# A second Strassen level for the S4 B22 product of three gate-and-up pairs

## The chip, the cores and the metric

One core of a Trainium2 chip. The metric is device time in microseconds; the kernel before takes 1020.71 us (median of three runs, 1020.18 to 1020.84). TensorE (PE) multiplies, VectorE (DVE) adds and splits, ScalarE (ACT) copies, splits and computes the gelu, SyncE (SP) issues loads, GpSimd (POOL) issues stores.

## The reference

`x` is 2048 x 640, in float32:

```python
g = _sigmoid((x * gate_w).sum(-1, keepdims=True))
y = Cr @ (x @ Hr.T) - Ci @ (x @ Hi.T)              # branch A: real part of a 2-D DFT, by matrices
b = (_gelu(x @ w_gate) * (x @ w_up)) @ w_down      # branch B: hidden size 1728
out = g * y + (1 - g) * b
```

## The kernel before

Each float32 factor is split into a high and a low float32r part (`high` on ACT, `low` on DVE, line 81), and one product of 128x128 by 128x512 is `mm3`: three matmuls, lines 89 to 91, high by high, high by low, low by high. All large products go through a Strassen-Winograd scheme: sums T1 to T4 of blocks of x, sums S1 to S4 of blocks of the weights, and sums of the partial results.

Gate and up of branch B work on the hidden blocks in pairs. `k = p` counts pairs, `f = 2p + 1` and `f + 1` are the two weight blocks of a pair. Pairs 2 to 5 run through the generator `whole_pair`. The names in it: `X[i, tp]` and `Z[i, tp]` are PSUM banks for weight block i and half tp of the rows of x; `s1`, `s2` are tiles of 128x512 in SBUF with gate results and state, `s5` (two buffers) holds the up part. `va`, `xa_`, `ve`, `xe` and `za`, `ze` are the banks of a second Strassen level, in which the 2 x 2 grid of (weight block, half of x) is taken as a matrix again: J = 1 and 2 for A11 and A12, J = 3 for S1 T1. For a level J, `WP[J]` holds its weights (a11, a12, a22 and the sums s1 to s4), `b[J]` its x blocks (b11, b21, b22 and t1 to t4); t1, t2, t4 come from DRAM (`xtd[J]`) by `load_cross(J, i)` into tiles `xx`, t3 replaces a block of x that is no longer used. `m(ps, J, w, x)` is one product of a second level, `prod` two (the block's two halves), `fifth` one. A `seed` copies a bank into another (ACT, line 461), a `plus` adds (DVE, line 548), `state` copies X into s2 (ACT, line 137). After `gated_out` (gelu, multiply, stores: lines 707 to 714) and `up_out` (lines 720 to 726) a block's results go to DRAM.

The order of PE's work is that of the program (`in_order(PE)`). DVE and ACT take theirs from the framework's list scheduling, in program order as far as inputs are ready by its reckoning, plus edges made by hand: `mark(key)` remembers the last instruction, `behind(key)` puts the newest one behind it on its engine. The generator yields numbers u, and the loop around it puts the rest between: `chain_parts` (sums and splits of the S weights: tiles ws, wd), `fifth_parts` (sums s1 to s4 for J = 3: tiles fs, fh), `plain_parts` (tile wp), `next_pair` (the next pair's vs, vl, ve, vq), `extras` (sums for a later stage, and logits of the gate: tiles dr, xz), loads. `next_pair`'s first sums and the extras are behind the mark "dve".

Most SBUF tiles (4 KB a partition) rotate through one pool of 46 slots, of which the x blocks keep some 32; a load waits on SP until a slot is free. PSUM has eight banks. After pair 5 the K stage multiplies by w_down: step i needs the splits kl, kb..0l and kb..1l of step i.

## Time and profile before

| | |
|---|---|
| median of the runs | 1020.71 us |
| profiled execution, its own time | 1020.78 us |
| its span | 1019.0 us |
| PE busy | 1013.6 us, 4488 matmuls |
| DVE, ACT, POOL busy | 811.6, 494.9, 145.5 us |
| pairs 3, 4, 5 | from 190.2, 237.1 and 284.0 us on |
| K stage | from 331.1 us on |

In a timeline a row gives start and length in us, engine, line, operation, the tile written and those read (buffer numbers left out: `s` is any of s1, s2, s5, `px` any X bank), the shape, and in brackets how long the engine was idle before and who ended that. Rows overlap, since an engine begins an instruction while the one before ends, so the cost of one is best read from start to start.

### The profile page before, as it was taken

The page shows a single profiled execution, that of the slowest core. Times are in us where ns is not written, and L with a number is a line of the kernel's source. Part 1 is how long each engine was busy: PE and PEld are TensorE (multiplying, and loading weights), DVE is VectorE, ACT ScalarE, POOL GpSimd, SP SyncE. Part 2 cuts the span into 40 slices and gives each one's busy share as a digit, 9 for nine tenths or more (in the row PEclk, how much of TensorE's full clock was granted, in tenths as well). Part 3 has the DMA queues.
Part 4 walks back from the last instruction along what each step waited for, and adds up shares of the span by engine and source line. Part 5 has one row for each costly group of instructions (what it writes and reads, how often), then busy time and mean ns, then how long its engine had stood idle before and what let it go on. Part 6 is the DMA issues. An engine that isn't in the chain of part 4 may idle for free.

```text
span 1019.0 us, 13152 instructions
## 1 busy us (share of the span) xinstructions
PE 1013.6 (99%) x4488; PEld 835.3 (82%) x4488; DVE 811.6 (80%) x1148; ACT 494.9 (49%) x660; POOL 145.5 (14%) x259
## 2 busy tenths in 40 slices
PE   9999999999999999999999999999999999999998
PEld 7888888888888888887888888888888888888887
DVE  6988887978778939967898976878687769797777
ACT  5455455545365637456455443434443345455431
POOL 0113130212123100100010022002100200021013
PEclk9999999999999999999999999999999999999999
DMA  8358797959699978877866579657965878697748
GB/s 283 138 189 300 267 331 235 350 198 351 208 344 365 359 257 275 294 245 259 294 222 219 198 265 333 237 199 264 336 210 195 303 245 289 249 388 219 258 97 132
DMA packets 87795, 265.01 MB, mean 260 GB/s; under 512 B 11216, under 2 KB 19440, under 8 KB 87728
## 3 DMA queue, kind: packets, MB, share of 16 engines
q1 hardware_dynamic: 65392, 194.47, 56.0%
q0 software_dynamic: 22192, 69.50, 20.1%
q8 instruction: 35, 0.57, 0.2%
q14 instruction: 32, 0.26, 0.1%
q10 hardware_dynamic: 144, 0.20, 0.1%
HBM read 194.38 MB, written 69.75 MB: 259 GB/s over the span
## 4 chain that ended last, share of the span: by engine, by line
PE 87%; issue 8%; DVE 2%; POOL 1%; DMA 1%; ACT 1%; POOLq 0%; ACTq 0%; DVEq 0%
PE pX L89 4%; PE pX L90 4%; PE pX L91 4%; PE pL L89 3%; PE pL L90 3%; PE pL L91 3%; PE px L89 3%; PE px L91 3%; PE px L90 3%; PE pZ L89 2%; PE pZ L90 2%; PE pZ L91 2%; PE pV L89 2%; PE pV L90 2%; PE pV L91 2%
## 5 line engine op out<-in xcount | busy, mean ns | idle before, releaser
L78 ACT ACTIVATE ch<-csa 128x1024 fp32r<-128x1024 f32 x32 | 34.0, 1063 | 75.2 <-DVE csa L868 66.9
L81 DVE TENSOR_TENSOR cl<-cra,ch 128x1024 fp32r<-128x1024 f32 x32 | 39.2, 1224 | 28.8 <-ACT ch L78 23.4
L78 ACT ACTIVATE ch<-cra 128x1024 fp32r<-128x1024 f32 x32 | 33.9, 1060 | 57.0 <-PE pY L90 19.2
L81 DVE TENSOR_TENSOR cl<-crb,ch 128x1024 fp32r<-128x1024 f32 x32 | 39.1, 1223 | 13.5 <-ACT ch L78 11.4
L90 PE MATMUL pL<-cl,xah 128*128 128x512 f32 x128 | 49.8, 389 | 0.0
L91 PE MATMUL pL<-ch,xal 128*128 128x512 f32 x128 | 49.8, 389 | 0.0
L89 PE MATMUL pL<-ch,xah 128*128 128x512 f32 x128 | 49.3, 389 | 0.0
L78 ACT ACTIVATE ch<-crb 128x1024 fp32r<-128x1024 f32 x32 | 33.8, 1057 | 22.6 <-DVE cl L81 7.8
L81 DVE TENSOR_TENSOR cl<-csb,ch 128x1024 fp32r<-128x1024 f32 x32 | 39.2, 1225 | 2.0 <-ACT ch L78 0.5
L81 DVE TENSOR_TENSOR cl<-csa,ch 128x1024 fp32r<-128x1024 f32 x32 | 39.1, 1221 | 1.7 <-PE pL L90 0.7
L78 ACT ACTIVATE ch<-csb 128x1024 fp32r<-128x1024 f32 x32 | 34.0, 1064 | 10.3 <-DVE csb L871 6.4
L350 POOL DMA_DIRECT2D hA<-s x48 | 26.2, 546 | 83.1 <-DVE s L708 52.2
L707 ACT ACTIVATE s<-s 128x512 f32<-128x512 f32 x20 | 12.7, 633 | 49.1 <-DVE s L548 33.0
L81 DVE TENSOR_TENSOR kl<-kw,kh 128x1024 fp32r<-128x1024 f32 (+1 forms) x26 | 31.5, 1211 | 3.6 <-ACT kh L78 3.6
L78 ACT ACTIVATE kh<-kw 128x1024 fp32r<-128x1024 f32 (+1 forms) x26 | 27.2, 1046 | 7.9 <-DVE kw L926 4.7
L981 POOL DMA_DIRECT2D out<-ks x12 | 6.5, 543 | 167.1 <-DVE ks L980 166.5
L548 DVE TENSOR_TENSOR s<-s,px 128x512 f32<-128x512 f32 x12 | 8.2, 686 | 27.5 <-ACT s L630 25.9
L1343 POOL DMA_DIRECT2D uA<-c x8 | 4.3, 543 | 170.9 <-DVE c L1430 170.7
L350 POOL DMA_DIRECT2D hT<-s x48 | 26.0, 543 | 17.9 <-DMA hA<-s 3.1
L91 PEld LDWEIGHTS pL<-ch,xal 128*128 128x128 f32 x128 | 24.0, 188 | 5.0
L89 PEld LDWEIGHTS pL<-ch,xah 128*128 128x128 f32 x128 | 24.0, 188 | 5.0
L90 PEld LDWEIGHTS pL<-cl,xah 128*128 128x128 f32 x128 | 24.0, 188 | 5.0
(3089 smaller groups left out, 3471.4 us busy)
## 6 DMA issues: line engine op xcount, KB each, us to landing
cra<-in_ct SPq DMA_DIRECT2D x64, 512.0 KB, 4.0
crb<-in_ct SPq DMA_DIRECT2D x64, 512.0 KB, 4.8
xx<-xtd SPq DMA_DIRECT2D x42, 512.0 KB, 6.1
hA<-s POOLq DMA_DIRECT2D x48, 256.0 KB, 5.9
hT<-s POOLq DMA_DIRECT2D x48, 256.0 KB, 6.4
kr<-hA SPq DMA_DIRECT2D x24, 512.0 KB, 7.9
kr<-hT SPq DMA_DIRECT2D x24, 512.0 KB, 6.3
ux<-uA SPq DMA_DIRECT2D x24, 512.0 KB, 6.0
```

Source lines behind the costliest of these rows:

```text
L78: nc.scalar.activation(hi, raw, AF.Copy)
L81: nc.vector.tensor_tensor(lo, raw, hi.bitcast(F32), op=ALU.subtract)
L89: nc.tensor.matmul(ps, lh, rh, start=first, stop=False, skip_group_check=True)
L90: nc.tensor.matmul(ps, lh, rl, start=False, stop=False, skip_group_check=True)
L91: nc.tensor.matmul(ps, ll, rh, start=False, stop=last, skip_group_check=True)
L350: nc.gpsimd.dma_start(to[:, i], src)
L548: tt(a, a, c, op=ALU.add)
L707: nc.scalar.activation(s2, s2, AF.Gelu_apprx_tanh)
L981: nc.gpsimd.dma_start(out[2 * tp + t, e], src)
L1343: nc.gpsimd.dma_start(to[:, i], src)
```

## The change

For p = 3, 4, 5 the part of `whole_pair` behind u = 23 is replaced by `inner_two`. There S4 B22 gets a second level too, J = 4: its weights are S4 of both blocks and new sums `inner_parts(p, 4)`; its x blocks are block (2, 2) and its sums `xtd[4]`, loaded by three more `load_cross` a pair. The banks of J = 3 (`Z`) go on accumulating J = 4's products after s5 has taken its part, and two banks `wa`, `we` hold the shared partial results, which DVE adds into s2. To free two banks, the first block's A22 T4 product and the first half of `up_out` (`up_first`) run earlier; the copies of X into s5 therefore come first. p = 2 makes the sums for J = 4 (`cross_loads(4)`, `cross_sums(4)`, a split at u = 65), and its extras move. In pair 5 `gate_rows` moves from u = 47 to 56.

```diff
-    def fifth_parts(p, W0, W1):
-        a, b = W0["raw"], W1["raw"]
+    def inner_parts(p, J, W0, W1):
+        a, b = W0["raw"][J], W1["raw"][J]
...
+        streamed(3, "S1")
+        if p > 2:
+            yield from inner_two(p, m, prod, fifth, plus, gelu, state, streamed, X, Z, s1, s2)
+            return
...
+    def inner_two(p, m, prod, fifth, plus, gelu, state, streamed, X, Z, s1, s2):
+        f = 2 * p + 1
+        prod(X[0, 1], 0, "S3", "T3", 1)
+        za, ze = bank(f"pza{p}"), bank(f"pze{p}")
+        m(za, 3, "a11", "b11", True)
+        Z[0, 0] = seed(za, f"pz00{p}")
+        gelu(s1[1, 1])
+        m(ze, 3, "s1", "t1", True)
+        sz = copy(ze, f"sz{p}")
+        prod(X[1, 0], 1, "S2", "T2", 0)
+        state(1, 0)
+        yield 29
+        m(Z[0, 0], 3, "a12", "b21")
+        m(za, 3, "s2", "t2")
+        Z[0, 1] = seed(za, f"pz01{p}")
+        prod(X[1, 1], 1, "S2", "T2", 1)
+        state(1, 1)
+        mark("state")
+        yield 32
+        s5 = sumtile(f"s5{f}")
+        for tp in range(2):
+            nc.scalar.activation(s5[:, tp], X[0, tp], AF.Copy)
+            behind("state")
+        fifth(Z[0, 0], 0, "u5", 1, 0)
+        prod(X[0, 0], 0, "A22", "T4", 0)
+        fifth(X[0, 0], 0, "u5", 0, 0)
+        plus(s5[:, 0], Z[0, 0])
+        mark("dve")
+        up_first(X[0, 0], 0, p, s1[0, 0])
+        yield 36
+        m(Z[0, 1], 3, "s4", "b22")
+        m(za, 3, "s3", "t3")
+        Z[1, 0] = seed(za, f"pz10{p}")
+        plus(za, sz)
+        Z[1, 1] = za
+        prod(X[0, 1], 0, "A22", "T4", 1)
+        fifth(X[0, 1], 0, "u5", 0, 1)
+        up_first(X[0, 1], 1, p, s1[0, 1])
+        fifth(Z[0, 1], 0, "u5", 1, 1)
+        plus(Z[0, 1], sz)
+        plus(s5[:, 1], Z[0, 1])
+        mark("dve")
+        yield 41
+        m(Z[1, 0], 3, "a22", "t4")
+        streamed(4, "S4")
+        wa = bank(f"pwa{p}")
+        m(wa, 4, "a11", "b11", True)
+        plus(s2[0, 0], wa)
+        m(Z[0, 0], 4, "a12", "b21")
+        fifth(Z[0, 0], 0, "D", 1, 0)
+        plus(s2[0, 0], Z[0, 0])
+        yield 47
+        we = bank(f"pwe{p}")
+        m(we, 4, "s1", "t1", True)
+        gated_out(0, p, 0, s2[0, 0], s5[:, 0])
+        up_last(0, p, s1[0, 0], s2[0, 0], s5[:, 0])
+        m(wa, 4, "s2", "t2")
+        plus(s2[0, 1], wa)
+        m(Z[0, 1], 4, "s4", "b22")
+        fifth(Z[0, 1], 0, "D", 1, 1)
+        plus(s2[0, 1], we)
+        yield 50
+        plus(s2[0, 1], Z[0, 1])
...
+        gated_out(1, p, 0, s2[0, 1], s5[:, 1])
+        up_last(1, p, s1[0, 1], s2[0, 1], s5[:, 1])
+        yield 52
+        prod(X[1, 0], 1, "S3", "T3", 0)
+        plus(s51[:, 0], X[1, 0])
+        m(wa, 4, "s3", "t3")
+        for tp in range(2):
+            plus(s2[1, tp], wa)
+        plus(s2[1, 1], we)
+        yield 56
...
+        m(Z[1, 0], 4, "a22", "t4")
+        fifth(Z[1, 0], 1, "D", 1, 0)
+        plus(s2[1, 0], Z[1, 0])
+        gated_out(0, p, 1, s2[1, 0], s51[:, 0])
+        yield 59
...
+    def up_first(X, tp, k, s1, second=0):
         tt(s1, s1, X, op=ALU.mult)
         keep(hA[tp][k], 2 * second, s1)
...
+                    if p == 2:
+                        xc[4] = cross_loads(4)
...
-                    todo = extras(1, 2)
+                    todo = extras(1, 2 if p > 2 else 0)
+                if u == 29 and p == 2:
+                    t3[4] = cross_sums(4, xc[4])
...
+                    if p > 2:
+                        load_cross(4, 1)
+                        load_cross(4, 2)
+                        todo = extras(not more, 2)
...
+                if u == 41 and p > 2:
+                    load_cross(4, 4)
...
+                if u == 65 and p == 2:
+                    split(Bs[1][2, 2][0][:, 0], Bs[1][2, 2][1][:, 0], t3[4])
...
                     if u == 47:
+                        load_k(0)
+                    if u == 56:
                         gate_rows()
-                        load_k(0)
```

## The prediction

> **What bounds the kernel now.** I read the page first, then the busy time by stretches over the five pairs, then the timelines of PE, ACT and DVE inside one pair. A pair is one pass of `whole_pair`; p = 4 runs from 237.10 to 284.02 us and stands for p = 3 and 5 as well. The page:

> ```profile
> span 1019.0 us, 13152 instructions
> PE 1013.6 (99%) x4488; PEld 835.3 (82%) x4488; DVE 811.6 (80%) x1148; ACT 494.9 (49%) x660; POOL 145.5 (14%) x259
> ```

> The profiled execution took 1020.78 us, 0.07 over the median of 1020.71. TensorE is occupied throughout; the question is what a few matmuls less are worth in the stretch where they go. The stretches (columns: stretch, length, then busy time with the count for PE, weight loads, DVE, ACT, POOL; clock, DMA share, GB/s):

> ```profile
> 190.20:237.10 46.90, 46.90 (x208) 38.84 (x207) 37.42 (x75) 24.08 (x42) 9.21 (x18) 1.00 0.79 270
> 237.10:284.00 46.90, 46.90 (x208) 38.85 (x207) 37.43 (x75) 24.07 (x42) 9.21 (x18) 1.00 0.79 274
> ```
> ```profile
> 252.40:259.00 6.60, 6.60 (x31) 5.47 (x30) 0.03 (x1) 3.34 (x6) 0.00 (x0) 1.00 0.58 199
> 237.10:252.40 15.30, 15.30 (x69) 12.68 (x68) 15.01 (x32) 12.33 (x23) 2.89 (x6) 1.00 1.02 365
> 265.10:286.50 21.40, 21.40 (x96) 17.72 (x95) 19.15 (x36) 7.12 (x12) 7.07 (x13) 1.00 0.80 276
> ```

> In a pair PE never stops: 207 matmuls in 46.92 us, 0.2267 us each at full clock, so one product (`mm3`, three matmuls) is 0.68 us. DVE looks free by 9.5 us a pair, but not evenly: it is full for the first 15.3 us, empty for 6.6 us, and again nearly full for the last 19 us and 2.5 us beyond the pair's end. I count time from a pair's first matmul (R) and products from 0; product n starts at R 0.68 n.

> **The gain.** Counting `mm3` calls, a pair has 69 products before and 68 in `inner_two`: S4 B22 had 8 and takes 7. Three pairs (p = 3, 4, 5) lose 9 matmuls: 9 x 0.2267 = -2.04 us. That is 0.2%, the least that a measurement of this kernel can tell from no change; the ceiling of the change is the edge of it.

> **A new wait of PE in each pair.** `s5[:, tp] = copy(X[0, tp])` is put behind `state(1, 1)` on ACT, and `state(1, 1)` waits for product 33. `prod(X[0, 0], "A22")` overwrites what that copy reads and is product 35; only `fifth(Z[0, 0])` lies between. The rows of such a hand-over, in p = 2, where PE waits for an ACT copy, and of ACT's start behind PE in p = 4:

> ```profile
> 157.80 0.39 PE L91 MATMUL px<-xT12h,ws5l 128*128 128x512 f32 x1
> 158.09 0.50 PE L89 MATMUL px<-xT03h,ws5h 128*128 128x512 f32 x1
> 158.42 0.39 PE L90 MATMUL px<-xT03l,ws5h 128*128 128x512 f32 x1
> ```
> ```profile
> 156.91 0.63 ACT L551 ACTIVATE s<-s 128x512 f32<-128x512 f32 x1 [0.93 <-DVE s L548]
> 157.45 0.58 ACT L137 ACTIVATE s<-px 128x512 f32<-128x512 f32 x1
> 157.93 0.62 ACT L551 ACTIVATE s<-s 128x512 f32<-128x512 f32 x1
> ```
> ```profile
> 237.56 0.39 PE L91 MATMUL pva<-x021h,ve 128*128 128x512 f32 x1
> ```
> ```profile
> 237.98 0.58 ACT L461 ACTIVATE pv<-pva 128x512 f32<-128x512 f32 x1 [3.40 <-PE pva L91]
> 259.01 0.69 DVE L548 TENSOR_TENSOR s<-s,px 128x512 f32<-128x512 f32 x1 [6.59 <-ACT s L630]
> ```

> ACT starts 0.42 us after the start of the last matmul (237.56 to 237.98); two ACT instructions that need not wait start 0.48 apart (157.45, 157.93); a copy takes 0.6; PE starts 0.05 after its end (157.45 + 0.58 to 158.09), and the matmul after that is 0.33 behind instead of 0.23. So from the last matmul of product 33: 0.42 + 0.48 + 0.6 + 0.05 = 1.55 us, where PE would have gone on after 4 x 0.2267 = 0.91. Stall 0.64 + 0.1 + some hundredths for the next few matmuls = 0.8 us; with copies 0.68 apart (as where each waits for its own product) 1.0; with the shortest rows 0.7. Three pairs: +2.4 (2.1 to 3.0). This alone eats the gain.

> **DVE.** `inner_two` has 16 `plus` where 10 stood: wa, we and Z come to s2 in ten adds instead of four. `inner_parts` for J = 4 adds four 128x128 sums and one 128x512 `low`. Rows for these and for the places where DVE's order meets PE's:

> ```profile
> 243.67 0.28 DVE L296 TENSOR_TENSOR fs<-ws10r 128x128 f32<-128x128 f32 x1
> 243.87 0.28 DVE L297 TENSOR_TENSOR fs<-ws9r,ws10r 128x128 f32<-128x128 f32 x1
> ...
> 245.08 0.68 DVE L81 TENSOR_TENSOR wp<-wa,wp 128x512 fp32r<-128x512 f32 x1
> 245.68 0.69 DVE L548 TENSOR_TENSOR px<-px,sx 128x512 f32<-128x512 f32 x1
> ...
> 264.51 0.69 DVE L548 TENSOR_TENSOR s<-s,px 128x512 f32<-128x512 f32 x1 [0.34 <-ACT s L646]
> 265.11 0.42 DVE L278 TENSOR_TENSOR vs<-wa 128x256 f32<-128x256 f32 x1
> ...
> 284.96 0.68 DVE L720 TENSOR_TENSOR s<-s,pxa 128x512 f32<-128x512 f32 x1
> 285.56 0.42 DVE L244 TENSOR_TENSOR ws11r<-wb,wa 128x256 f32<-128x256 f32 x1
> 285.89 0.69 DVE L723 TENSOR_TENSOR s<-s,s 128x512 f32<-128x512 f32 x1
> 286.49 0.42 DVE L245 TENSOR_TENSOR ws11r<-wa,wb 128x256 f32<-128x256 f32 x1
> ```
> ```profile
> 247.30 0.39 PE L89 MATMUL pv<-x05h,wp 128*128 128x512 f32 x1
> ```

> Start to start a 128x512 operation costs 0.60 (245.08, 245.68), a 128x128 one 0.20. Added a pair: 6 x 0.60 + 4 x 0.20 + 0.60 = 5.0 us, to 42.4 of some 47. [...]

> What decides is where this work can lie. The preparation of the next pair (vs, vl, ve, wp) and the gate logits are held behind the marked add to s5. Before, that add is the row at 264.51, R 27.4, and vs follows at once. In `inner_two` the mark stands on `plus(s5[:, 1], Z[0, 1])` behind product 43: R 0.68 x 44 + 0.2 + 0.6 for the add before it = 30.7, with the stall 31.5, its end 32.1. Product 68 (the next pair) starts at 46.24 + 0.8 = 47.0, so 14.9 us are left where 18.9 were. The work behind the mark was 21.4 us less 2.25 of idle = 19.1 (row 265.10:286.50), or 18.8 without the next pair's ws11r; of the added adds six lie there and two multiplications (`up_first`) have moved ahead of it: 18.8 + 4 x 0.60 = 21.2. DVE is done with the pair 6.3 us after its end, where before it was 2.1 (286.49 less the 0.34 of ws11r, against 284.02): 4 us later. The idle 6.6 us earlier in the pair can't take it, since the inputs don't exist yet.

> Who waits: the first products of the next pair need banks, of which six are free in time. The split of wp (row 245.08, ready by 245.7, R 8.6) is read by product 15 (247.30, R 10.2; its low part 0.45 later, 10.65): 2.0 us of slack. DVE is full before it, so the 4 us come through, with 0.8 for the new sums: 8.6 + 4.2 + 0.8 = 13.6 at worst, a stall of 2.9. A little later the gelu behind `s + sv` precedes the copy of X[0, 0] on ACT, which product 22 waits for; in p = 2 that add came late by about 1.6 us and cost PE 0.17 (row 158.09), and here it is late by 4.2 + 0.8 + 0.6. Both together: some 5.5 less 2.0 = 3.5 us per boundary. The idle stretch then clears it. It happens where a changed pair is followed by another: p = 3 to 4 and 4 to 5, +7.0 us. Bounds: 0 (if DVE's list puts the six stores' subtractions, 3.6 us, and the logits, 1.5, after the next pair's splits) and 2 x 5.5 = 11. I take 3.5, since DVE's rows show no idle moment ahead of product 15.

> **Into the K stage.** p = 5 has no next pair but the first K splits, and `gate_rows` moves from u = 47 to 56 with two logits more behind the mark.

> ```profile
> 334.37 1.22 DVE L81 TENSOR_TENSOR kb0010l<-kr,kb0010h 128x1024 fp32r<-128x1024 f32 x1
> 335.50 1.22 DVE L81 TENSOR_TENSOR kb0011l<-kr,kb0011h 128x1024 fp32r<-128x1024 f32 x1
> ```
> ```profile
> 337.90 0.39 PE L89 MATMUL kX<-kb0010h,kh 128*128 128x512 f32 x1
> ```

> kb0010l is done at 335.6, 2.5 us before its use (338.12). With 3 to 4 us more ahead of it: +1.0 (0 to 2.5). The transpose of `gate_rows` now waits in PE's order behind product 56 for two logits and a sigmoid: +0.2 (0 to 1.5).

> **The rest.** p = 2 keeps its products; `cross_sums(4)` (four adds, two splits, about 4.1 us) fits its idle stretch, but two slots for its loads come before wp, and its late split delays p = 3 by 0.6 beside the 0.8 and 0.6 of J = 4, about what p = 2 showed: together +0.4 (0 to 1.5). Nine loads of 512 KB more: SP is past its waits when they are due; 0 if the slots come in time (rival below). ACT gains 0.6 us a pair beside 22 idle: 0. The pool DMAs are four more, in p = 2 alone: 0.

> Sum: -2.04 + 2.4 + 7.0 + 1.0 + 0.2 + 0.4 = +9.0, 1020.7 + 9.0 = 1029.7 us.

> **Rivals.** (1) DVE keeps up, because its list lets urgent splits pass: -2.04 + 2.4 + 0.4 = +0.8, 1021.5 us. For it: 4.6 us of DVE's pair would still be idle. Against: before the mark it has nothing to do with them. (2) Faster, the other side: the copies of X[0, tp] are off PE's path and DVE keeps up: 1018.7 us. It decides if ACT ends the copy within 0.91 us of product 33's last matmul; the rows give 1.50. [...] (3) The loads of xx for J = 4 come late: their slots are those that this pair's earlier tiles free.

> ```profile
> xx<-xtd SPq DMA_DIRECT2D x42, 512.0 KB, 6.1
> ```

> A load takes 6.1 us, nine products. Product 49 needs its tile; a slot freed by product 43 (the last use of wp) would give it at 53: 2.7 us a pair, 8.1 in all, with the 0.8 of rival 1: 1029.6, or less where only one pair is hit. For it: every one of the 13 or so rotating slots is taken there, with one more for the new splits. Against: the xx tiles of J = 3 are free by product 31.

> **Chances.** DVE-bound boundaries 0.58 (its own range 1025 to 1034), rival 1 0.23, rival 2 0.09, rival 3 0.10. Slower by over 0.2% (over 1022.75): 0.58, 0.09 of rival 3, and 0.03 of rival 1: 0.70. Within: 0.20 of rival 1, 0.04 of rival 2, 0.01 of rival 3: 0.25. Faster: 0.05 of rival 2. Range 1020.6 to 1034: it leaves out rival 2 and the sum of all upper bounds.

> **What would show it.** In the profile after: 4479 matmuls; a gap of 0.7 to 1.0 us before the first `px<-xT04h,wp` of p = 3, 4, 5, ended by ACT; DVE without idle from the mark to the next pair's idle stretch, its last stores 6 us into the next pair; PE waiting for DVE's wp, or ACT's copy, in the first 16 us of p = 4 and 5, and for kb0010l. The prediction is wrong if DVE's idle stretch in p = 3 to 5 has moved rather than shrunk, if the pairs 4 and 5 last no longer than 47.1 us, or if PE stops at product 48 or 49 for a DMA.

## The result, and the profile after

The changed kernel takes 1042.45 us (median; 1041.65 to 1044.69), the kernel before 1020.47 beside it: ratio 1.0218, 95% interval 1.0204 to 1.0233. It is 22 us slower, where 9.0 were forecast (range to 1034). The profiled execution took 1042.61 us.

The page of the changed kernel, its span and engine line, and the busy time by stretches (pair 1, then p = 2, 3, 4, 5, then the rest; columns as before):

```profile
span 1040.8 us, 13216 instructions
PE 1021.1 (98%) x4479; PEld 837.1 (80%) x4479; DVE 831.7 (80%) x1188; ACT 497.6 (48%) x666; POOL 147.6 (14%) x263
```
```profile
95.60:143.60 48.00, 47.97 (x212) 39.35 (x211) 40.07 (x74) 23.21 (x39) 13.79 (x25) 1.00 0.84 292
143.60:196.90 53.30, 49.36 (x208) 39.79 (x207) 41.66 (x78) 26.24 (x46) 11.14 (x20) 0.97 0.78 271
196.90:241.90 45.00, 44.50 (x196) 36.51 (x195) 36.86 (x77) 23.12 (x41) 6.82 (x14) 1.00 0.82 285
241.90:294.40 52.50, 48.81 (x205) 39.24 (x205) 42.63 (x86) 24.50 (x43) 9.24 (x18) 0.97 0.79 273
294.40:351.50 57.10, 51.87 (x215) 41.42 (x214) 44.88 (x88) 28.71 (x47) 11.06 (x21) 0.94 0.98 361
351.50:1040.80 689.30, 684.57 (x3047) 564.94 (x3045) 548.85 (x683) 322.35 (x378) 80.24 (x137) 1.00 0.76 254
```

The nine matmuls are gone (4479), yet PE is *busy* 7.5 us longer, and two things that the page of before did not have are in these rows: PE stands still for some us in p = 2, 4 and 5 (stretch less PE's busy time: 3.9, 3.7 and 5.2 us), and the granted clock is 0.97, 0.97 and 0.94 there. The length of a pair, from its first matmul to the next pair's, with its share of both (a matmul at half clock takes 0.427 us from start to start where it took 0.227):

| pair | before | after | matmuls after | PE's stops in it | half clock |
|---|---|---|---|---|---|
| p = 2 | 47.12 | 53.32 | 207 | 1.70, 2.53 | 3.41 |
| p = 3 | 46.92 | 45.03 | 195 | 0.66 | 0 |
| p = 4 | 46.92 | 52.47 | 204 | 0.66, 0.72, 2.80 | 3.41 |
| p = 5 | 47.07 | 57.09 | 214 | 0.66, 1.98, 2.81, 0.37, 0.44 | 6.83 |

A stop here is the distance between two matmuls' starts less the usual 0.23. The counts differ because the last three products of p = 3 and p = 4 (X[1, 1]'s A22 T4) now run behind the first ones of the next pair; p = 3, 4 and 5 have 613 together, 204 or 205 each. The K stage has 1.1 us more, in stops of 0.8 and 0.35.

PE's own list of waits names the causes (columns: what waits, for what; us in all, times, longest). All four lines are of the pairs:

```profile
PE pv L91 <- DVE wp L81: 5.3, 2, 2.6
PE pv L89 <- ACT wp L78: 3.9, 3, 1.8
PE pz L89 <- ACT s L654: 2.4, 1, 2.4
PE px L89 <- ACT s L705: 1.5, 3, 0.5
```

`DVE wp` is the wait at product 15 of p = 4 and 5. PE and DVE there, in p = 4:

```profile
254.94 0.50 PE L89 MATMUL pv<-x05h,wp 128*128 128x512 f32 x1 [0.56 <-ACT wp L78]
255.28 0.39 PE L90 MATMUL pv<-x05l,wp 128*128 128x512 f32 x1
258.31 0.50 PE L91 MATMUL pv<-x05h,wp 128*128 128x512 f32 x1 [2.63 <-DVE wp L81]
...
259.12 0.63 PE L91 MATMUL px<-xx,vq 128*128 128x512 f32 x1
259.55 0.63 PE L89 MATMUL pva<-x15h,wp 128*128 128x512 f32 x1
```
```profile
248.52 0.69 DVE L818 TENSOR_TENSOR s<-s,s 128x512 f32<-128x512 f32 x1 [0.66 <-DMA hT<-s]
...
255.35 0.28 DVE L296 TENSOR_TENSOR fs<-ws10r 128x128 f32<-128x128 f32 x1
...
257.37 0.28 DVE L299 TENSOR_TENSOR fs<-ws9r,fs 128x128 f32<-128x128 f32 x1
257.57 0.68 DVE L81 TENSOR_TENSOR wp<-wa,wp 128x512 fp32r<-128x512 f32 x1
```

The low part of wp ends at 258.25, 16.3 us after the pair's first matmul (241.95), where it ended at 8.6 before; DVE has no idle moment in the 9 us ahead of it. Two rows on, the matmuls take 0.43 us from start to start: the clock has gone to half for 3.41 us.

The stop in p = 2 is another one. ACT's row there:

```profile
177.47 0.42 ACT L78 ACTIVATE vq<-wa 128x256 fp32r<-128x256 f32 x1 [4.17 <-DMA wa<-in_wf]
177.79 0.58 ACT L654 ACTIVATE s<-pz 128x512 f32<-128x512 f32 x1
```
```profile
178.43 0.50 PE L89 MATMUL pz<-x122h,ws5h 128*128 128x512 f32 x1 [2.37 <-ACT s L654]
```

ACT stood 4.17 us at the split of vq, whose load had not landed, and the copy that PE needed stood behind it. SP issues the two loads of the next pair's weights at line 235, and vq reads the second. They went out at 167.37 and 167.9, and before at 156.72 and 161.1, so the first was ten us and the second six us earlier in the pair then (a row has both, with the start of the first):

```profile
167.37 0.97 SPq L235 DMA_DIRECT2D wa<-in_wf  x2
```
```profile
156.72 4.74 SPq L235 DMA_DIRECT2D wa<-in_wf  x2
```

SP's own list of waits names what held the first of them: 7.5 us for a slot, until DVE's split (xU4l) had read the x blocks that p = 2 now loads for J = 4.

```profile
SPq L235 <- DVE xU4l L81: 7.5, 1, 7.5
```

The other stop of p = 2, 1.70 us, is at product 15. ACT's split of wp ran at 154.82, 11.2 us after the pair's first matmul, behind copies and a gelu; before, it ran at 150.32, 7.3 us after it, ahead of them:

```profile
154.82 0.62 ACT L78 ACTIVATE wp<-wa 128x512 fp32r<-128x512 f32 x1
```
```profile
150.32 0.62 ACT L78 ACTIVATE wp<-wa 128x512 fp32r<-128x512 f32 x1
```

### The profile page after: what moved, and what is told of

It reads as the page before. It is cut to its first block, busy times and chain, and to the rows that moved or that the text cites. A ratio compares the mean times of both kernels' runs of the same rounds, so it can differ in the third digit from the quotient of the medians.

```text
span 1040.8 us, 13216 instructions
## 1 busy us (share of the span) xinstructions
PE 1021.1 (98%) x4479; PEld 837.1 (80%) x4479; DVE 831.7 (80%) x1188; ACT 497.6 (48%) x666; POOL 147.6 (14%) x263
## 4 chain that ended last, share of the span: by engine, by line
PE 43%; issue 38%; DVE 6%; DMA 5%; POOL 5%; ACT 2%; POOLq 0%; DVEq 0%; ACTq 0%
DMA hT<-s 2%; POOL uT L1470 2%; PE px L89 2%; POOL uA L1470 2%; PE px L90 2%; PE px L91 1%; PE pX L89 1%; PE pX L91 1%; PE pX L90 1%; PE pZ L89 1%; PE pZ L90 1%; PE kL L90 1%; PE pZ L91 1%; PE kL L91 1%; PE kX L89 1%
## 5 line engine op out<-in xcount | busy, mean ns | idle before, releaser
L81 DVE TENSOR_TENSOR cl<-cra,ch 128x1024 fp32r<-128x1024 f32 x32 | 39.1, 1222 | 30.4 <-ACT ch L78 23.4
L91 PE MATMUL pL<-ch,xal 128*128 128x512 f32 x128 | 49.8, 389 | 0.0
L90 PE MATMUL pL<-cl,xah 128*128 128x512 f32 x128 | 49.8, 389 | 0.0
L89 PE MATMUL pL<-ch,xah 128*128 128x512 f32 x128 | 49.3, 389 | 0.0
L81 DVE TENSOR_TENSOR cl<-crb,ch 128x1024 fp32r<-128x1024 f32 x32 | 39.1, 1222 | 11.8 <-ACT ch L78 10.0
L81 DVE TENSOR_TENSOR cl<-csb,ch 128x1024 fp32r<-128x1024 f32 x32 | 39.2, 1225 | 2.9 <-ACT ch L78 1.2
L81 DVE TENSOR_TENSOR cl<-csa,ch 128x1024 fp32r<-128x1024 f32 x32 | 39.0, 1220 | 1.5 <-PE pL L90 0.7
L81 DVE TENSOR_TENSOR kl<-kw,kh 128x1024 fp32r<-128x1024 f32 (+1 forms) x26 | 31.4, 1209 | 3.4 <-ACT kh L78 3.4
L91 PEld LDWEIGHTS pL<-ch,xal 128*128 128x128 f32 x128 | 24.0, 188 | 5.0
L90 PEld LDWEIGHTS pL<-cl,xah 128*128 128x128 f32 x128 | 24.0, 188 | 5.0
L89 PEld LDWEIGHTS pL<-ch,xah 128*128 128x128 f32 x128 | 24.0, 188 | 5.0
L550 DVE TENSOR_TENSOR s<-s,pz 128x512 f32<-128x512 f32 x18 | 12.3, 683 | 17.9 <-ACT s L705 17.0
## 6 DMA issues: line engine op xcount, KB each, us to landing
cra<-in_ct SPq DMA_DIRECT2D x64, 512.0 KB, 4.0
crb<-in_ct SPq DMA_DIRECT2D x64, 512.0 KB, 4.9
xx<-xtd SPq DMA_DIRECT2D x51, 512.0 KB, 6.2
kr<-hA SPq DMA_DIRECT2D x24, 512.0 KB, 7.2
kr<-hT SPq DMA_DIRECT2D x24, 512.0 KB, 7.1
ux<-uA SPq DMA_DIRECT2D x24, 512.0 KB, 6.3
```

The lines of the kernel that those rows point to most:

```text
L81: nc.vector.tensor_tensor(lo, raw, hi.bitcast(F32), op=ALU.subtract)
L89: nc.tensor.matmul(ps, lh, rh, start=first, stop=False, skip_group_check=True)
L90: nc.tensor.matmul(ps, lh, rl, start=False, stop=False, skip_group_check=True)
L91: nc.tensor.matmul(ps, ll, rh, start=False, stop=last, skip_group_check=True)
L550: tt(a, a, c, op=ALU.add)
```

## The experiments

Theory: the stops are separate faults of order (a late load in p = 2, a copy put behind `state`, DVE's backlog ahead of wp), and the half clock follows them. Rivals: they hide one another; or the total of DVE's work sets the time. All ratios are to the kernel before.

**Pair 2's preparation alone.** inner_two is not called, pairs 3 to 5 run as before; p = 2 makes the sums for J = 4 as in the change.

```diff
-        if p > 2:
-            yield from inner_two(...)
-            return
```

> Pairs 3 to 5 run as before (no J = 4, no loads and no split for it); pair 2 still loads the x blocks and makes cross_sums(4), and the extras and gate_rows stand where the change put them. Theory (the 6.2 us that pair 2 lost come from this preparation alone: two slots taken ahead of wp, the next pair's loads pushed back): pair 2 lasts 52 to 54 us again with PE stopping before product 15 and before S4 of Z[0, 1], pairs 3 to 5 last 46.9 to 47.5, total 1026 to 1028. Rival (pair 2 lost its time to something of inner_two or of the loads for J = 4): pair 2 at 47.1, total 1020 to 1021.

Measured: 1025.8 (1.0052 [1.0036, 1.0069]). p = 2 lasts 50.97 us, pairs 3 to 5 46.92, 46.92 and 47.07 as before; both stops of p = 2 are there (1.70 and 1.75), with no half clock. So the preparation, costed at +0.4 together with p = 3, costs 4 to 5 us by itself.

**The same preparation later.** The loads of J = 4's blocks go behind those of the next pair's weights, the sums to u = 41.

```diff
-                    if p == 2:                 # u == 10
-                        xc[4] = cross_loads(4)
...
                         nraws = next_raws(p + 1)   # u == 32
+                    if p == 2:
+                        xc[4] = cross_loads(4)
```

> Pair 2's loads of the x blocks come behind the next pair's weights (u = 32), cross_sums(4) at u = 41. Theory (the loads' two slots and their order ahead of wp and of the next weights stop PE in pair 2): both stops in pair 2 go, pair 2 lasts 47 to 48 us, total 1036 to 1038, unless the 4 us of DVE for the sums, now behind the mark, make wp of pair 3 late by 2 to 3 us, which would bring back 2 to 5. Rival (pair 2 is slow through the number of its DVE and ACT instructions, wherever they stand): pair 2 at 52 or more, 1042.

Measured: 1036.24 (1.0147 [1.0132, 1.0163]). p = 2 lasts 47.58, and of its stops one of 0.30 is left. That settles the cause: the same loads and sums at another place cost p = 2 0.5 us and not 6.2.

**The copies into s5 first**, ahead of `prod(X[1, 1], "S2")` and `state(1, 1)`.

```diff
+        s5 = sumtile(f"s5{f}")
+        for tp in range(2):
+            nc.scalar.activation(s5[:, tp], X[0, tp], AF.Copy)
         prod(X[1, 1], 1, "S2", "T2", 1)
         state(1, 1)
```

> The copies of X[0, tp] into s5 stand ahead of S2 T2 of X[1, 1] and of state(1, 1), with no edge behind state. Theory (the copy behind state stops PE 0.77 us in each of pairs 3 to 5, in the place of nothing else): the 0.88 us steps before the first px<-xT04h are gone, total 2.3 us less, 1040.1; the waits for wp in pairs 4 and 5 stay, since the mark and the pair's end both come 0.8 earlier. Rival (DVE sets the length of the pairs, so a wait saved there comes back as a longer wait for wp): 1042 to 1042.5.

Measured: 1038.91 (1.0176 [1.0158, 1.0194]). The three stops of 0.66 are gone; p = 4's stops at product 15 are longer by 0.5 in sum (0.84, 2.81 and 0.37 after 0.72 and 2.80), p = 5's shorter by 1.6 (0.77 and 2.81 after 1.98, 2.81 and 0.37). The term was 2.4; the median moved by 3.5, in a run that spreads over 1036.7 to 1041.1.

**Both together.**

> Both earlier repairs together: the copies of X into s5 come first, and pair 2's loads and sums for J = 4 come late. Theory (the costs are separate waits and add): 1036.2 less 3 x 0.8 = 1033.8, within 1031 to 1035.5, with the waits for wp (about 3 us each in pairs 4 and 5) still there. Rival (the 0.8 us steps only hide later waits, which then grow): 1036.

Measured: 1034.17 (1.0119 [1.0098, 1.0139]). p = 2 and 3 are at full pace (47.15 and 44.22), and what is left is DVE's wp, as long as ever:

```profile
PE pv L91 <- DVE wp L81: 5.3, 2, 2.6
...
PE pv L89 <- ACT wp L78: 1.0, 2, 0.6
```

So the two nearly add: 3.5 for the copies and 6.2 for pair 2, and 8.3 together.

**Six adds less on DVE**, in the change as it was made. The adds of wa and we to s2 are left out, so those parts are missing from the output.

```diff
-        plus(s2[0, 0], wa)
...
-        for tp in range(2):
-            plus(s2[1, tp], wa)
-        plus(s2[1, 1], we)
```

> The six adds of wa and we into s2 are left out (s2 lacks them); the products, loads, splits and the order are those of the change. Theory (DVE's list behind the mark is too long by some 4 us, and wp of the next pair comes late for that): the waits of PE before product 15 of pairs 4 and 5, 3.5 and 4.8 us, shrink to under 1.5 each, the stretches at half clock there go, total 1029 to 1033. Rival (slots and loads hold wp back: one slot more in use and three loads more a pair): waits and clock as in the change, 1041 to 1043.

Measured: 1033.19 (1.012 [1.0104, 1.0135]). Pairs 4 and 5 last 48.71 and 50.43, half clock is left in p = 2 alone, and the wait for wp falls from 2.8 to 0.5 us each. But 2.37 us at a pv bank's copy appear in p = 5: the miss of this expectation, and the first sign that the backlog moves on to the next instruction in the row.

**Less for DVE by other means.** On top of both repairs, first vs's and dr's sums on GpSimd; then the second mark left out; then an inner_two with seeds, old order up to product 38.

```diff
-            tt(sm[:, k], v, w, op=op)
+            nc.gpsimd.tensor_tensor(sm[:, k], v, w, op=op)
```

> As the run with both repairs, but vs's sums (four of 128x256 a pair, 0.33 us each from start to start on VectorE) and the four sums into dr run on GpSimd: VectorE has 2.6 us a pair less behind the mark, with the same instructions in all. Theory (VectorE's row of work ahead of wp decides): the wait for wp in pairs 4 and 5 shrinks from some 4 us to 1.4 or less each, and with it the half clock goes: 1033.8 less 5 to 8 = 1026 to 1029. Rival (something else holds wp, a slot or a load): no change, 1033.8. Third: GpSimd is so slow on these sums that vh comes late instead: a wait for vs, vh or vl in place of wp, 1034 or more.

Measured: 1039.13 (1.0165 [1.0145, 1.0185]). None of the three as it was put. The wait for wp falls to 2.2 each, but not by as much as VectorE was relieved, and two others come: 3.5 us for a pv copy, 4.3 for adds of s2. GpSimd takes 0.7 to 1.4 us for a sum of 128x256 (VectorE 0.42), and the stores stand in the same queue; those into hT land 7.5 us after their issue in the median, where it was 7.0 in the run with both repairs, and VectorE stands at a tile that one is still reading, with ScalarE's splits behind it and the pv copy behind those:

```profile
L280 POOL TENSOR_TENSOR vs<-vs,wa 128x256 f32<-128x256 f32 x3 | 4.1, 1379 | 0.0
```
```profile
191.24 0.69 DVE L815 TENSOR_TENSOR s<-s,s 128x512 f32<-128x512 f32 x1 [1.32 <-DMA hT<-s]
```
```profile
198.06 0.31 ACT L78 ACTIVATE wd<-wb 128x128 fp32r<-128x128 f32 x1 [4.14 <-DVE wb L248]
```
```profile
PE pwa L89 <- DVE s L549: 4.3, 2, 2.2
PE pv L91 <- DVE wp L81: 4.3, 2, 2.2
PE pv L89 <- ACT pv L461: 3.5, 2, 3.3
```

```diff
         plus(s5[:, 1], Z[0, 1])
-        mark("dve")
         yield 41
```

> As the run with both repairs, but the second mark on VectorE (the add behind product 43) is left out, so that the next pair's sums need only be behind the add behind product 35, 6 us earlier. The work on VectorE stays the same. Theory (the mark is what puts 21 us of work into 15): VectorE begins the next pair's sums in the pauses ahead of product 43, the wait for wp shrinks by 1 to 4 us each: 1025 to 1031. Rival (VectorE is simply too full, whatever the order): 1033 to 1035. It may also go wrong: the sums put ahead of the adds to s5 and s2 keep the banks of Z taken, and TensorE waits for a bank inside the pair.

Measured: 1032.44 (1.0103 [1.0087, 1.0119]); the waits for wp are 2.8 us as before it. Within 2 us of the run it came from, and the spread of that one (1031.9 to 1035.7) covers it. The run does not try its theory, though: vs's first sum in p = 3 starts 32.9 us after the pair's first matmul, where it was 32.1 with the mark, and in p = 4 at 40.5 instead of 39.4. So this mark is not what holds the sums where they stand; what an earlier start would bring stays open.

```diff
+        wa = bank(f"pwa{p}")
+        m(wa, 4, "a11", "b11", True)
+        W00 = seed(wa, f"pw00{p}")
...
+        plus(s2[0, 0], W00)
```

> Another inner_two, of the same products: J = 4 has its own banks with seeds (three copies and one more on ScalarE) instead of being added into s2 from wa and we, so that VectorE gets two 128x512 adds more than before a pair and not six; the order of products up to the mark is the old one, so the mark stands where it stood before, and only the first block's A22 T4 comes forward, behind it. Pair 2's sums come late. Theory: behind the mark VectorE has 18.8 + 2 x 0.6 = 20 us in 18.2, late by 1.8 instead of 4 to 6, which the 2.0 us of slack take up: 1036.2 less 2.4 (no wait at product 35) less 9 (waits for wp and half clock) = 1021 to 1025. Rival (TensorE gets new waits for banks, since W00, W01 and W10 take banks that X00 and X01 free only after VectorE's multiplication): 1 us in each of three pairs or more, 1025 to 1030.

Measured: 1029.89 (1.0082 [1.0061, 1.0103]). As built it adds only J = 4's banks to s2 and leaves out S1 T1's share there, which a whole version would have to add, so it has four adds fewer than that one. The wait for wp is 0.50 in p = 4 and gone in p = 5, and another has come:

```profile
PE pv L89 <- ACT pv L462: 5.5, 2, 3.9
```
```profile
290.14 0.69 DVE L812 TENSOR_TENSOR s<-s,s 128x512 f32<-128x512 f32 x1 [3.08 <-DMA hA<-s]
292.07 0.69 DVE L814 TENSOR_TENSOR s<-s,s 128x512 f32<-128x512 f32 x1 [1.24 <-DMA hT<-s]
```

DVE stands 4.3 us at two subtractions that write a tile which a store is still reading; ws and wb, on which ScalarE's row rests, are behind them. Neither theory had this.

**Order instead of amount.** On top of both repairs, with the same work:

```diff
                 if u == 3:
-                    Ws.append({})
+                    Ws.append(plain_parts(f + 1, raws[1][0]))
```

> As the run with both repairs, but the split of the second block's wp is called ahead of that pair's S sums and of the sums for J = 3 and 4 (u = 3 and not 10). The work on each engine is the same. In the run with both repairs VectorE had 17 instructions for S and fs, some 6 us, ahead of wp's low part, which TensorE waited for 0.6 + 2.8 us in pairs 4 and 5, with half clock behind it. Theory (VectorE's backlog is 4 to 6 us, and it comes out at what stands last): the wait for wp goes, but the adds to X (px<-px,sx) and the copy behind them are then late for product 22, 1 to 2.5 us a pair: 1026 to 1031. Rival (the order alone was wrong, the backlog has slack elsewhere): pairs 4 and 5 at 47 us, 1022 to 1025. Second rival (the total of VectorE's work sets the pair): no change, 1034.

Measured: 1028.41 (1.0084 [1.0066, 1.0102]), no half clock. The wait for wp is gone and the copies of X, behind the adds to X, are late by 2.1 and 0.9 us a pair:

```profile
PE px L89 <- ACT s L137: 5.5, 4, 2.0
```

> As the run with wp's split first, but the two logits (0.75 us each from start to start on VectorE) that stand behind the mark in pairs 3 to 5 are done in the same pair's idle stretch, with the other two. VectorE has 1.5 us less behind the mark, nothing is left out. Theory (backlog behind the mark): 1.5 us less wait in pairs 4 and 5 and in the first K step each, where it waits: 1 to 4 us less than the run with wp first, 1022 to 1028. Rival (what TensorE waits for is not the backlog): the same as the run with wp first.

```diff
-                    todo = extras(1, 2 if p > 2 else 0)
+                    todo = extras(1, 4 if p > 2 else 0)
...
-                        todo = extras(not more, 2)
+                        todo = extras(not more, 0)
```

Measured: 1026.73 (1.006 [1.0044, 1.0076]). The stops at px shrink from 3.0 to 1.7 a pair; a stop for pv (1.2 and 1.8) appears, since DVE now meets the store of hA:

```profile
240.54 0.69 DVE L814 TENSOR_TENSOR s<-s,s 128x512 f32<-128x512 f32 x1 [1.95 <-DMA hA<-s]
```

The gate logits' transpose no longer stops PE (0.44 in the change): its logits are done early.

> As the run with the logits in the idle stretch, but the second block's S sums and the sums and splits for J = 3 come at u = 13 and 16, and those for J = 4 at u = 16 and 23, so that the adds to X and s1 pass them on VectorE. The work is the same. Theory (TensorE waits for whatever urgent operation stands behind not yet urgent ones on VectorE and ScalarE): the adds to X come 3 us earlier, waits in pairs 4 and 5 under 0.5 us, 1019.5 to 1023. Rival (total work): no change against the run before it. It may go wrong at ScalarE, where three gelus of the last pair now stand ahead of the first seeds of the next: up to 1 us in each of pairs 3 to 5.

```diff
-                    parts = [chain_parts(f + i, raws[i], Ws[i]) for i in range(2)]
+                    parts = [chain_parts(f, raws[0], Ws[0])]
...
+                if u == 13:
+                    parts.append(chain_parts(f + 1, raws[1], Ws[1]))
+                    parts.append(inner_parts(p, 3, *Ws))
```

Measured: 1031.47 (1.0107 [1.0091, 1.0123]): a miss. The copy of px is later still, by 2.0 us in pairs 4 and 5 and 0.8 in pairs 2 and 3, with half clock behind each of the two of 2.0; the stops for pv (1.2 and 1.3) stay. The sums that went behind the adds to X let ScalarE start ws10h only now, right ahead of the copies (the last row, the first of two):

```profile
254.79 1.04 ACT L78 ACTIVATE ws10h<-ws10r 128x1024 fp32r<-128x1024 f32 x1
255.74 1.07 ACT L137 ACTIVATE s<-px 128x512 f32<-128x512 f32 x2
```

> As the run with the logits in the idle stretch, but the last three subtractions of the second half (into hT, from s and from t1) are issued in the next pair, behind wp and the S sums, and the sums for J = 4 come at u = 16. In the run before, VectorE stood for 1.95 us in pair 4 at a subtraction whose tile a store (hA<-s) was still reading, with all of the next pair's splits behind it. The work is the same. Theory (what is late is whatever stands behind such an operation on VectorE): 1.95 us of standing and 1.2 us of subtractions leave the way of the adds to X, the waits for pv (1.2 and 1.8 us in pairs 4 and 5) go and those for px shrink from 1.7 to about 1 us a pair: 1021.5 to 1024. Rival (a store that is late only stops VectorE a little later): 1026 to 1027. The side that would beat the kernel before, 1020 or less, needs every wait in pairs 3 to 5 to be under 2 us in sum, which this does not bring.

```diff
-            up_out(X[1, tp], tp, p, 1, s1[1, tp], s2[1, tp], s51[:, tp])
+            up_out(X[1, tp], tp, p, 1, s1[1, tp], s2[1, tp], s51[:, tp], tail if tp else None)
...
                 if u == 7:
                     parts[0]()
+                    for do in tail:
+                        do()
```

Measured: 1023.56 (1.0026 [1.0016, 1.0036]). DVE stands no more, the stops for pv are gone, and pairs 3 to 5 have one stop left, of 1.72 us, in each of p = 4 and 5:

```profile
250.94 1.07 ACT L78 ACTIVATE ws10h<-ws10r 128x1024 fp32r<-128x1024 f32 x1
251.89 1.16 ACT L553 ACTIVATE s<-s 128x512 f32<-128x512 f32 x2
252.96 1.07 ACT L137 ACTIVATE s<-px 128x512 f32<-128x512 f32 x2
```

The copy that PE waits for is the third row; a split and two gelus that nobody waits for yet are ahead of it.

> As the run with the held-back subtractions, but in pairs 3 to 5 ScalarE copies X[0, 0] and X[0, 1] into s2 ahead of two gelus and of ws10h (gelu of s1[0, 1] and s1[1, 0] behind the second copy, the split of the second block's S sums at u = 23). In the run before, TensorE's only stops in pairs 4 and 5 were 1.72 us each ahead of px<-xT03h,ws9h, at those copies, which stood behind ws10h (0.95 us) and two gelus (1.07). The work is the same. Theory (TensorE waits for the urgent operation that stands behind less urgent ones; with no stop left the change is worth its nine matmuls): the two stops shrink by 1.4 to 1.7 us each, 1023.5 less 3 = 1019.5 to 1021.2. Rival (the backlog is simply passed on once more): the gelus, the Z seeds or s5 come late instead, 1022.5 to 1024.

```diff
+            mark("state")
+            gelu(s1[0, 1])
+            behind("state")
...
                 if u == 16:
-                    parts[1]()
...
                 if u == 23 and p > 2:
+                    parts[1]()
                     WP[4] = parts[3]()
```

Measured: 1038.01 (1.0165 [1.0146, 1.0183]): a miss. The stop at px is gone, and 4.3 us and more at ws10h stand in its place: called at u = 23, it takes its slots behind the logits, and ScalarE waits for VectorE's last use of a tile by line 943, which is a logit.

```profile
261.19 1.06 ACT L78 ACTIVATE ws10h<-ws10r 128x1024 fp32r<-128x1024 f32 x1 [4.08 <-DVE z L943]
```

> As the run with the held-back subtractions, with nothing moved but the two gelus on ScalarE: in pairs 3 to 5 they stand behind the copies of X[0, 0] and X[0, 1] into s2 and no longer ahead of them; ws10h and its slots stay where they were (in the last run its late slot made TensorE wait 4.3 us and more for ws10h, while the stop at px<-xT03h was gone). Theory: the stop of 1.72 us shrinks by the gelus' 1.07 us to 0.65 in each of pairs 4 and 5: 1023.5 less 2.1 = 1021.4, within 1020.8 to 1022. Rival (the backlog comes out elsewhere): 1022.5 to 1023.6.

The diff is that of the run before it without the part on `parts[1]`. Measured: 1023.27 (1.0026 [1.0017, 1.0035]). The stop shrinks by 1.04 us (1.07 expected), and 0.5 us come out at a Z seed in p = 4 and 0.4 at an add that reads X at the start of p = 5; in the median 0.3 us are left of it, less than the spread of the runs. That is the rival's range, and its reason. This is the fastest version of the change, and it is still 2.6 us slower than the kernel before; none beat it.

## Why the prediction was wrong, by its steps

The direction and most of the mechanisms were right, the sum was not. Of the some 22 us in the span:

- **The gain** (-2.04): right, 4479 matmuls.
- **The wait at product 35** (+0.8 each, +2.4): right. PE's stop is 0.66 and the start-up of the next matmul 0.11, so 0.77; the run with the copies first has no stop there.
- **"DVE is done with the pair 6.3 us after its end" and "some 5.5 less 2.0 = 3.5 us per boundary"**: the mechanism is shown, by the wait for DVE's wp and by its going with six adds less or with wp first; 3.5 were measured in p = 4 and 5.2 in p = 5, 8.7 against 7.0 (0.2 of it is the half clock in the step listed as 0.37). In p = 4 wp came 7.7 us later after the pair's start and not 5.0, for two reasons that the prediction had not: 2.0 us because PE begins the next pair ahead of the last three products, and 0.66 because DVE stood at a tile that a store was reading. In p = 5 it came 8.9 us later; there DVE stood 1.85 us at two such tiles.
- **"p = 2 ... together +0.4 (0 to 1.5)"**: this step failed. The preparation costs 3.9 us of p = 2 alone and 6.2 in the whole change, half clock included. The prediction saw the two slots ahead of wp and DVE's four adds; it did not follow what else is moved on SP. The next pair's weights come through the same queue and pool, the first of their loads waited 7.5 us for a slot and the one for vq went out six us later in the pair, and ACT stood 4.17 us at vq with the copy for PE behind it. Rival 3 asked the right question (is a load late for want of a slot) at the wrong load.
- **No term for the clock**: this step was missing. 13.65 us of the pairs run at half clock, some 6 us of the 22 (3.41 us each cost 1.7; p = 5's two windows, with 2 us of standing in them, 2.5). Before there was no such stretch, so no row of it could price it, and a stop was counted at its own length alone.
- **Into the K stage** (+1.0) and the transpose (+0.2): 1.1 and 0.44, inside their bounds, but the first by luck. At kb0010l, the term's own place, PE stops 0.35; the other 0.82 are at a matmul of kb0000h into kL, which one of DVE's multiplications (line 824) released, a wait that the prediction had not.
- Of the rivals, (1) and (2) are refuted by the 5.3 us at wp, and (3) as it was put by the stops of p = 3, 4 and 5, none of which a load ended. For (2): PE was busy for 99% of the span before the change and DVE for 80%, and still the time went up by 22 us with nine matmuls fewer.

The terms as measured: pairs 2 to 5 +6.2, -1.9, +5.6 and +10.0 (the table), pair 1 and ahead +0.5 (the first pair's start moves by more than that from run to run, 94.9 to 96.8), K +1.1, the end +0.3: 21.8, the difference of the spans.

What the runs settle: with the same products and the same amount of work, order alone is worth 19 of the 22 us (1042.45 to 1023.27). What stays open is whether the last 2.6 us can be had, and the gain of 2.04 with them; each reordering from 1026.7 on but the one to 1023.56 brought out another stop, and in the fastest version DVE is busy for 41.9 of the 48.1 us of p = 4 and 45.5 of the 49.8 of p = 5. No run shows a version without stops.

## What to carry to other kernels

Price a stop of TensorE by what may follow it, not by its length alone: in the change one of 1.70 us (p = 2) was followed by a window of half clock, which cost another 1.7 us. When work is added to a nearly full pipeline, follow every queue that it passes (here the load queue and the pool's rotation), and look on each engine for the urgent operation that stands behind less urgent ones: moving that one costs no work, and here such moves gave back 19 us in all, where six adds less gave 9. Neither is sure: after both, part of the backlog came out at the next instruction in the row. A change that saves TensorE 0.2% and adds 5 us to an engine with 9 to spare in 47 begins with more to lose than to win.

## What the runs showed of the hardware

```profile
251.90:255.66 3.76, 3.20 (x13) 2.00 (x12) 3.76 (x12) 2.96 (x6) 0.55 (x1) 1.00 0.96 350
255.66:259.07 3.41, 0.78 (x4) 0.67 (x4) 3.41 (x11) 2.22 (x4) 0.00 (x0) 1.00 1.04 332
259.07:262.49 3.42, 3.42 (x9) 2.67 (x8) 3.37 (x6) 1.96 (x4) 0.00 (x0) 0.50 0.92 316
262.49:265.90 3.41, 3.41 (x16) 2.79 (x15) 3.38 (x8) 2.44 (x5) 0.00 (x0) 1.00 0.67 224
```

In the rows above the window ahead of the slow one has 0.78 of 3.41 us busy. Over the profiled executions of all these kernels I summed PE's standing (starts more than 0.44 us apart, less 0.23) in each window at full clock from 10 to 1000 us of the span: in all 18 windows with 1.96 us or more of it the next window was at half clock, in none of 34 with 0.70 to 1.69 us, and in 2 of 8 between (1.70 to 1.93; the two stood 1.70, so no sharp point is shown). So in these traces a window idle by little more than half (1.96 of 3.41 us) was enough. In the change PE stood 1.70, 2.65 and 2.85 us in the windows ahead of the three stretches of half clock, and 1.27 at most in any other window at full clock from 10 to 1000 us. A stop of 2.53 us in p = 2 went free: the grid cut it into 1.25 and 1.27. So the time of this kernel depended on where its stops fell in the grid: with the preparation alone both stops (1.70 and 1.75) went free, and in the whole change one of them (1.70) did not.
